# Five chunks of a chain of matrix products by Strassen's scheme: seven block products in place of eight

## The chip, the cores and the metric

The kernel runs on one core of a Trainium2 chip. The metric is the device time of one execution in microseconds. The kernel before takes 239.56 us, the median of three runs from 239.36 to 239.72.

A core has five engines with a queue each, worked off in order: TensorE (PE) multiplies matrices, VectorE (DVE), ScalarE (ACT) and GpSimd (POOL) work on elements, SyncE (SP) issues transfers. PE writes to PSUM, which has eight banks of 512 fp32 columns. DVE and ACT copy results from there to SBUF.

## The reference

```python
def _attn_ref(q, k, v):                      # each (8, 8, 576, 64)
    q_s = softmax of q over the last axis
    k_s = softmax of k over the 576 positions
    kv = np.einsum('bhsd,bhse->bhde', k_s, v)
    return np.einsum('bhsd,bhde->bhse', q_s, kv)

def _moe_ref(x, w1, w2, w3, w_out):          # x (4608, 512); w1, w2 (512, 1024)
    a = x @ w1
    b = x @ w2
    h = a * b @ w3                           # w3 (1024, 1024)
    return h @ w_out                         # w_out (1024, 512)
```

The attention's result, as 4608 rows of 512, is the `x` of the second part. Softmax is written here in words; inputs and result are fp32.

## The kernel before

The matrix products run on f16 operands and accumulate in fp32. Since nothing stands between the last two products, the kernel first folds the weights: `W3O` is w3 times w_out, scaled, 1024 by 512, kept as 8 tiles of 128 rows. The output is then (a * b) times `W3O`.

**Chunks.** The 4608 rows are done in nine chunks of 512. Chunk c, below 8, holds 512 of batch c's 576 rows; chunk 8 holds the 64 rows left over from each of the eight batches. The attention of batch b runs ahead of chunk b.

**Attention of batch b.** The steps for k are the maximum (`kmx`, then `cba`, `cbx`, `cb`), the subtraction `ksub` and the exponential `kexp`; for q, in two parts of five and four row groups, the maximum `qmx`, `qsub`, `qexp`, the sum `qsm`, `qeps`, the reciprocal `qrc`, the scaling `qn` and a transpose, mostly by DMA (`qd`). `vc` casts v. PE makes the kv product (`kv`) and the chunk's x (`xm`, `xt`), which `xs` and `xts` copy out. `ksub`, `qsub` and `qn` mostly run on POOL.

**A chunk.** It consists of eight units u. In each, PE makes `up.1.c.0.u` (x times w2) and `up.0.c.0.u` (x times w1), each 4 matmuls of 512 columns into a bank of the ring `pab`, which has four. `bs` copies the first one's bank to SBUF as f16, on ACT or DVE, and frees it; `ab` (line 799, DVE) multiplies the second one's bank with that copy into the f16 tile `ab` and frees the second bank. So `up.0` of unit u+2 waits for `ab` of unit u. Chunks 0 and 1 do this in two halves, with 8 matmuls of 256 columns per step. Then come four steps `down.c.tb` (line 806), one for each 128 rows: 8 matmuls of 512 columns with `ab` as the loaded weights and `W3O` streamed, into a bank of the ring `po`, which has two. `os` (line 810) copies the bank to the fp32 tile `osb` on ACT or DVE, and `st` (line 829) stores it with two DMAs from SP. Chunk 8's are lines 818 to 827, with the last step in two halves. The `down` steps of a chunk stand among the `up` steps of the next one or two.

**The order.** Every step has a name like `ab.4.0.5`. The string `ORDER` lists all 795 steps; they are emitted in that order, so each engine's queue has the order in which its steps stand there. `PICKS` names the engine of steps that could run on several. Both are fixed lists. Waits between engines follow from the data.

**The links.** Some steps of DVE and POOL are marked as users of a port that the two share: `ksub`, `qsub`, `qn`, `vc` on POOL, `qeps` on DVE and others. Where such a step is followed in `ORDER` by one of the other engine, `link` makes the later wait for the end of the earlier, though their data don't ask for it, but for steps with an index below `LINKED` alone, which is 580 and counted from 0. In the kernel before, step 580 is `bs.5.0.3`; POOL has six more steps behind it.

```python
            if s["port"] and i < LINKED:
                if held and held[0] != s["eng"]:
                    link(got[0], held[1])
                held = s["eng"], got[-1]
```

**Weights.** `w316` holds the f16 w3 until the weights are folded, in the first 50 us or so; `w3T` is the ring, two tiles deep, through which it goes transposed.

## Time and profile before

| | us |
|---|---|
| median of 3 runs | 239.56 |
| the profiled execution's span | 237.4 |
| PE busy in it | 230.1 |
| DVE busy | 180.3 |
| ACT busy | 121.7 |
| POOL busy | 110.0 |

The span runs from the first instruction to the last of one profiled execution; the time of a run is taken around it, and no time of its own was taken of the profiled one. The page gives for each group of instructions its line, engine, operation, what it writes and reads, the count, the busy time, the mean of one in ns, and the idle time of the engine ahead of them with what ended it. Matmuls are pipelined: the next begins before the last one's time is over, so their durations overlap. In the 40 slices a digit is the busy share of a slice in tenths. The chain of waits follows the work that ended last back to the start.

### The profile page before, as it was taken

To read this page: it belongs to the slowest core of one execution; us is meant where nothing else is said; L and a number is where in the kernel's file an instruction comes from. 1 tells how busy PE (TensorE), PEld (TensorE's weight loads), DVE (VectorE), ACT (ScalarE), POOL (GpSimd) and SP (SyncE) were. 2 spreads that over 40 slices of the span, in tenths; PEclk is the share of its full clock that TensorE was granted. 3 is DMA by queue.
4 is the path that set the end of the run, shared out by engine and by line. 5 is a ranking of instruction groups with operands and counts; after the bars stand their busy time and mean duration, and the time that the engine had idled before them with its cause. 6 is when DMAs were issued, how large, how long until landed. Compare 5 with 4: busy or idle time off the path is not lost.

```text
span 237.4 us, 4860 instructions
## 1 busy us (share of the span) xinstructions
PE 230.1 (97%) x1935; PEld 119.5 (50%) x1935; DVE 180.3 (76%) x277; ACT 121.7 (51%) x221; POOL 110.0 (46%) x73
## 2 busy tenths in 40 slices
PE   7889999999999999999999999999999999999994
...
DVE  2998699998998999998999798679566365326640
...
POOL 8234258469958899469673593338500000000000
...
DMA packets 38742, 46.51 MB, mean 196 GB/s; under 512 B 17088, under 2 KB 22976, under 8 KB 38720
## 3 DMA queue, kind: packets, MB, share of 16 engines
...
q8 instruction: 15, 0.25, 0.4%
q14 instruction: 7, 0.06, 0.1%
...
## 4 chain that ended last, share of the span: by engine, by line
PE 81%; DMA 8%; DVE 5%; POOL 4%; issue 1%; ACT 0%; POOLq 0%; ACTq 0%
PE pab L784 46%; PE po L806 22%; DMA w<-in_moe_w_dram 6%; PE po L457 4%; PE po L821 3%; PE pkv L549 2%; DMA qT<-en 2%; PE xm L667 1%; DVE qm L582 1%; POOL k L524 1%; PE w3t L445 1%; POOL en L619 1%; POOL w L406 1%; DVE ab L799 1%; DVE kmx L498 1%
## 5 line engine op out<-in xcount | busy, mean ns | idle before, releaser
L784 PE MATMUL pab<-x,w1sb 128*128 128x512 f16 (+1 forms) x320 | 65.9, 337 | 0.4 <-DVE kmx L499 0.4
L784 PE MATMUL pab<-x,w2sb 128*128 128x512 f16 (+1 forms) x320 | 66.0, 337 | 0.0
L799 DVE TENSOR_TENSOR ab<-pab,bsb 128x512 f16<-128x512 f32 x72 | 48.6, 682 | 20.2 <-PE pab L784 13.6
L806 PE MATMUL po<-W3O,ab 128*128 128x512 f16 x256 | 58.9, 379 | 0.0
L784 PEld LDWEIGHTS <-w1sb 128*128 128x128 f16 x352 | 34.2, 98 | 28.5 <-DMA w1sb<-in_moe_w_dram 0.6
L784 PEld LDWEIGHTS <-w2sb 128*128 128x128 f16 x352 | 33.5, 98 | 27.5 <-issue 0.7
L325 ACT CAST bsb<-pab 128x512 f16<-128x512 f32 x46 | 26.8, 582 | 35.8 <-PE pab L784 34.6
L524 POOL TENSOR_TENSOR k<-k,cb 128x1152 f32<-128x1152 f32 x12 | 31.4, 2628 | 16.4 <-issue 5.1
L806 PEld LDWEIGHTS <-ab 128*128 128x128 f16 x256 | 24.5, 98 | 28.5 <-issue 0.4
L587 POOL TENSOR_TENSOR q<-q,qm 128x1024 f32<-128x1024 f32 (+1 forms) x14 | 29.5, 2125 | 13.1 <-DVE rc L573 5.4
L325 ACT COPY osb<-po 128x512 f32<-128x512 f32 (+1 forms) x25 | 14.3, 571 | 40.3 <-PE po L806 26.8
L619 POOL TENSOR_TENSOR en<-eq,qr 128x1024 f16<-128x1024 f16 (+1 forms) x13 | 27.2, 2106 | 10.5 <-DVE qr L612 10.4
L582 DVE TENSOR_REDUCE qm<-q 128x20 f32<-128x1280 f32 (+1 forms) x16 | 21.2, 1340 | 3.6 <-DMA q<-in_q_dram 3.6
L325 DVE CAST bsb<-pab 128x512 f16<-128x512 f32 x26 | 17.6, 677 | 6.8 <-PE pab L784 6.3
L600 DVE TENSOR_REDUCE qr<-eq 128x20 f32<-128x1280 f16 (+1 forms) x16 | 21.5, 1341 | 1.5 <-ACT eq L595 1.4
L595 ACT ACTIVATE eq<-q 128x1280 f16<-128x1280 f32 (+1 forms) x16 | 18.5, 1161 | 4.8 <-DVE q L587 3.9
L532 ACT ACTIVATE ek<-k 128x1152 f16<-128x1152 f32 x16 | 18.2, 1163 | 3.8 <-POOL k L524 3.8
L489 DVE TENSOR_REDUCE km<-k 128x128 f32<-128x1152 f32 x8 | 16.9, 2149 | 0.0
L457 PE MATMUL po<-wosb,w3T 128*128 128x512 f16 x64 | 15.3, 379 | 0.5 <-DMA wosb<-in_moe_w_out_dram 0.5
L325 DVE COPY osb<-po 128x512 f32<-128x512 f32 x12 | 8.3, 688 | 9.1 <-PE po L806 7.9
L329 ACT ACTIVATE x<-xm 128x512 f16<-128x512 f32 x18 | 10.3, 597 | 6.4 <-PE xm L667 6.2
L325 ACT CAST v<-v 128x1152 f16<-128x1152 f32 x9 | 10.3, 1148 | 0.3 <-DMA v<-in_v_dram 0.3
...
## 6 DMA issues: line engine op xcount, KB each, us to landing
...
k<-in_k_dram SPq DMA_DIRECT2D x4, 1152.0 KB, 10.1
...
```

The costliest lines, as they stand in the source:

```text
L325: return [(nc.scalar.copy if eng == "ACT" else engine[eng].tensor_copy)(out=out, in_=in_)]
L457: nc.tensor.matmul(st["pf", ft], lhsT=st["w3T", ft][:, gt, :], rhs=wosb[:, gt, :], start=(gt == 0), stop=(gt == N_FT - 1))
L524: return [engine[eng].tensor_tensor(out=kb[:, two(hp), :, :], in0=kb[:, two(hp), :, :], in1=st["cb", b][:, two(hp), None, :].broadcast_to( ...
L532: nc.scalar.activation(out=st["ek", b][:, hp, :, :].rearrange("p j (i d) -> p i j d", i=2), in_=kb[:, two(hp), :, :], func=AF.Exp)
L582: dve.tensor_reduce(out=st["qm", b][:, :, j], in_=qb[:, :, j, :], axis=AX.X, op=ALU.max)
L587: return [engine[eng].tensor_tensor(out=qb[:, :, j, :], in0=qb[:, :, j, :], in1=st["qm", b][:, :, j, None].broadcast_to([P, HH, n, D]), op ...
L595: nc.scalar.activation(out=st["eq", b, p], in_=qb[:, :, j, :], func=AF.Exp)
L600: dve.tensor_reduce(out=st["qr", b][:, :, slice(*PARTS[p])], in_=st["eq", b, p], axis=AX.X, op=ALU.add)
L619: return [engine[eng].tensor_tensor(out=st["en", b][:, j, :, :].rearrange("p j h d -> p h j d"), in0=st["eq", b, p], in1=st["qr", b][:, :, ...
L784: nc.tensor.matmul(st["p", one, c, sub, u][:, a * (t1 - t0):(a + 1) * (t1 - t0)], lhsT=w[:, ct, fb * P:(fb + 1) * P], rhs=x()[:, ct, t0:t1 ...
L799: dve.tensor_tensor(out=st["ab", c][:, nf * u:nf * u + nf, t0:t1], in0=cut(st["p", 0, c, sub, u]), in1=cut(st["bsb", c, sub, u]), op=ALU.mult)
L806: nc.tensor.matmul(st["po", c, tb], lhsT=st["ab", c][:, ft, tb * P:(tb + 1) * P], rhs=W3O[:, ft, :], start=(ft == 0), stop=(ft == N_FT - 1))
```

## The change

In chunks 3 to 7 the product of `ab` (512 rows by 1024) with `W3O` (1024 by 512) is cut into blocks: `ab` by halves of its rows and of the 1024, `W3O` by halves of the 1024 and of its columns. In place of eight block products there are seven, by Strassen's scheme in its form with 15 additions.

- `sT.1` to `sT.4`: four sums of the weights' blocks, once, on POOL. They and the chunks' sums lie in `w316`, whose weights are no longer needed (`sums[0..3]` and `sums[4..7]`).
- `sa.c.1` to `sa.c.4`: four sums of blocks of `ab`, 128 partitions by 1024 f16, for each chunk, on POOL or DVE. sa.4.1 and sa.4.2 are on DVE; sa.3.3, sa.3.4, sa.4.3 and sa.4.4 are on POOL, sa.3.2 on DVE. sa.c.2 and sa.c.4 read what sa.c.1 and sa.c.2 wrote.
- `sp.c.1` to `sp.c.7`: the seven products, each 8 matmuls of 256 columns. Products 1, 6, 5 and 3 add up in one bank, 7 and 4 in a second, 2 has a third, all from the ring `po` with its two banks.
- `kept.c.1` to `kept.c.3`: the first bank's partial sums, copied out on ACT or DVE after products 1, 6 and 5, as fp32, through the ring `w3T`, which gets a third tile. The next product into that bank waits for the copy.
- `os.c.n`: the four blocks of the output. os.c.12 is a copy; the other three add a bank and a kept sum, on DVE.
- `st.c.n`: a block's store, two DMAs as before, with 256 columns of two row groups each.

An `ab` of chunk c waits for chunk c-2's products and sums, where it waited for its `down` steps. On PE at least two steps stand between a product and the next one that uses its bank. `ORDER`, 849 steps now, is another list from `vc.2.1` on (some 60 us into the run), and `PICKS` with it: `bs`, `xs` and others change engines here and there. `LINKED` stays 580; step 580 is now `qsub.7.1`, on POOL, the first step behind it that uses the port. The diff, with the part of `ORDER` around the end of chunk 4 alone, and without `PICKS`:

```diff
--- before.py
+++ after.py
@@ ORDER @@
...
-qrc.6.1 up.1.4.0.4 bs.4.0.4 up.0.4.0.4 up.1.4.0.5 bs.4.0.5 ab.4.0.4 up.0.4.0.5 ab.4.0.5 up.1.4.0.6
-bs.4.0.6 qmx.7.0 up.0.4.0.6 up.1.4.0.7 up.0.4.0.7 ab.4.0.6 up.1.5.0.0 up.0.5.0.0 bs.4.0.7 down.3.3
-up.1.5.0.1 qsm.6.0 st.3.1 ksub.6.1 kexp.6.1 kexp.6.0 qn.6.1 ab.4.0.7 st.3.0 v.6 vc.6.1 vc.6.0 kv.6
-k.7 st.2.3 os.3.3 down.4.0 down.4.1 st.3.2 st.3.3 qd.6.1 qeps.6.0 bs.5.0.1 kve.6 os.4.0 os.4.1
...
+up.1.4.0.1 ab.3.0.7 kv.5 bs.4.0.0 up.0.4.0.1 kmx.6.0 st.2.0 bs.4.0.1 ab.4.0.0 sa.3.1 up.1.4.0.2
+up.0.4.0.2 bs.4.0.2 up.1.4.0.3 kve.5 qd.5.0 qsub.6.0 qexp.6.0 bs.4.0.3 st.2.1 qmx.6.1 ab.4.0.1
+qd.5.1 cba.6 up.0.4.0.3 kv2.5 up.1.4.0.4 bs.4.0.4 ab.4.0.2 sT.3 xm.5.1 xm.5.0 ab.4.0.3 qsm.6.0
+qmx.7.1 xt.4 xs.5.1.1 xts.4.0 v.6 xs.5.1.0 xts.4.1 xs.5.0.1 up.0.4.0.4 up.1.4.0.5 ab.4.0.4 cbx.6
+sa.3.3 sa.3.2 sp.3.2 vc.6.0 k.7 st.2.2 sp.3.1 qsub.6.1 qmx.7.0 bs.4.0.5 qsub.7.0 up.0.4.0.5 vc.7.1
+up.1.4.0.6 kmx.7.1 kept.3.1 sp.3.6 ab.4.0.5 up.0.4.0.6 os.3.11 cb.6 kept.3.2 st.2.3 bs.4.0.6
+up.1.4.0.7 sp.3.5 bs.4.0.7 sa.3.4 ab.4.0.6 up.0.4.0.7 xs.5.0.0 kmx.7.0 sp.3.7 kept.3.3 os.3.22
+ksub.6.1 qexp.7.0 ksub.6.0 up.1.5.0.0 sp.3.3 up.0.5.0.0 ab.4.0.7 qexp.6.1 os.3.12 qsm.6.1 sp.3.4
+sa.4.1 bs.5.0.0 sp.4.1 sa.4.2 ab.5.0.0 kept.4.1 os.3.21 up.1.5.0.1 qeps.6.1 vc.6.1 up.0.5.0.1
+qsm.7.0 qrc.6.1 up.1.5.0.2 st.3.11 bs.5.0.1 sp.4.6 kexp.6.0 st.3.22 qeps.6.0 ab.5.0.1 up.0.5.0.2
+kept.4.2 qsub.7.1 qrc.6.0 cba.7 up.1.5.0.3 up.0.5.0.3 qn.6.1 sp.4.5 bs.5.0.2 ab.5.0.2 cbx.7 kept.4.3
+qd.6.1 sa.4.3 qn.6.0 sp.4.7 kexp.6.1 cb.7 sa.4.4 bs.5.0.3 up.1.5.0.4 kv.6 qexp.7.1 os.4.22
...
     pab_pool = ctx.enter_context(tc.tile_pool(name="pab", bufs=4, space=bass.MemoryType.PSUM))
     po_pool = ctx.enter_context(tc.tile_pool(name="po", bufs=2, space=bass.MemoryType.PSUM))
     att_pool = ctx.enter_context(tc.tile_pool(name="att", bufs=2, space=bass.MemoryType.PSUM))
-    plan = Plan({"pab": 4, "po": 2, "att": 2, "osb": 4, "eq": 4, "bsb": 4, "w3T": 2}, PICKS, ORDER)
+    plan = Plan({"pab": 4, "po": 2, "att": 2, "osb": 4, "eq": 4, "bsb": 4, "w3T": 3}, PICKS, ORDER)
 
     def p_ab():
         return pab_pool.tile([P, 512], F32, tag="pab", name="pab")
@@ -303,6 +311,7 @@
     w2sb = wght.tile([P, N_CT, Fd], F16)
     W3O = wght.tile([P, N_FT, C], F16)
     w316 = wght.tile([P, N_FT, Fd], F16)
+    sums = [w316[:, x, :].rearrange("p (f t) -> p f t", f=4) for x in range(N_FT)]
     wosb = work.tile([P, N_FT, C], F16, tag="ab", name="wosb")
 
     EVICT = 100.0
@@ -318,6 +327,7 @@
     XMS = 3
     DMAT = [[b > DMATS or (b, p) in DMATP for p in range(2)] for b in range(B)]
     SPLIT = [0, 1]
+    SEVEN = [3, 4, 5, 6, 7]
     SUBS = [[(0, 256), (256, 512)] if c in SPLIT else [(0, 512)] for c in range(B + 1)]
     engine = {"DVE": dve, "POOL": g_, "ACT": nc.scalar}
 
@@ -445,7 +455,7 @@
                 nc.tensor.transpose(st["w3t", ft][:, gt, :], w316[:, ft, gt::N_FT], ident16)
 
         def ev(eng):
-            st["w3T", ft] = work.tile([P, N_FT, P], F16, tag="w3T", name="w3T")
+            st["w3T", ft] = work.tile([P, N_FT, P], F16, tag="w3T", name="w3T", bufs=3)
             copy(eng, st["w3T", ft], st["w3t", ft])
 
         ring = "po"
@@ -763,6 +773,8 @@
               [("xt", b)], gives=[("xt", b)])
 
     XS = {}
+    DONE = {}
+    BANK = {1: 0, 6: 0, 5: 0, 3: 0, 2: 1, 7: 2, 4: 2}
 
     def QFREE(b):
         return [n for n in plan.steps if n[0] in ("qt", "qd") and n[1] == b]
@@ -832,6 +844,57 @@
                 nc.sync.dma_start(
                     out=out[b * S:(b + 1) * S, :].rearrange("(p j) c -> p j c", j=NJ)[:, j, :],
                     in_=st["osb", c, tb][i * HALF:(i + 1) * HALF, :])
+
+        def sums_of(i, eng):
+            a = st["ab", c]
+            a11, a12, a21, a22 = [a[:, 4 * f:4 * f + 4, 256 * t:256 * t + 256]
+                                  for t in range(2) for f in range(2)]
+            in0, in1, op = {1: (a21, a22, ALU.add), 2: (sums[4], a11, ALU.subtract),
+                            3: (a11, a21, ALU.subtract), 4: (a12, sums[5], ALU.subtract)}[i]
+            return [engine[eng].tensor_tensor(out=sums[3 + i], in0=in0, in1=in1, op=op)]
+
+        def product(i):
+            bank = BANK[i]
+            fresh = i in (1, 2, 7)
+            if fresh:
+                st["ps", c, bank] = p_o()
+            a, w = st["ab", c], W3O
+            left = {1: (a, 0, 0), 2: (a, 4, 0), 3: (sums[7], 0, 0), 4: (a, 4, 256),
+                    5: (sums[4], 0, 0), 6: (sums[5], 0, 0), 7: (sums[6], 0, 0)}[i]
+            right = {1: (w, 0, 0), 2: (w, 4, 0), 3: (w, 4, 256), 4: (sums[3], 0, 0),
+                     5: (sums[0], 0, 0), 6: (sums[1], 0, 0), 7: (sums[2], 0, 0)}[i]
+            for tb in range(2):
+                for ft in range(4):
+                    t, f0, t0 = left
+                    r, g0, c0 = right
+                    nc.tensor.matmul(
+                        st["ps", c, bank][:, tb * 256:tb * 256 + 256],
+                        lhsT=t[:, f0 + ft, t0 + tb * P:t0 + tb * P + P],
+                        rhs=r[:, g0 + ft, c0:c0 + 256],
+                        start=fresh and tb == 0 and ft == 0, stop=ft == 3, skip_group_check=True)
+
+        def kept(i, eng):
+            st["kept", c, i] = work.tile([P, 512], F32, tag="w3T", name="kept", bufs=3)
+            copy(eng, st["kept", c, i], st["ps", c, 0])
+
+        def block(n, eng):
+            st["osb", c, n] = work.tile([P, 512], F32, tag="osb", name="osb", bufs=4)
+            if n == 12:
+                copy(eng, st["osb", c, n], st["ps", c, 0])
+                return
+            i, bank = {11: (1, 1), 22: (3, 2), 21: (2, 2)}[n]
+            dve.tensor_tensor(out=st["osb", c, n], in0=st["ps", c, bank], in1=st["kept", c, i],
+                              op=ALU.add)
+
+        def store_block(n):
+            t0, c0 = n // 10 - 1, (n % 10 - 1) * 256
+            for i in range(2):
+                j = 4 * t0 + i
+                nc.sync.dma_start(
+                    out=out[c * S:(c + 1) * S, :].rearrange("(p j) c -> p j c", j=NJ)[
+                        :, j:j + 3:2, c0:c0 + 256],
+                    in_=st["osb", c, n][i * HALF:(i + 1) * HALF, :].rearrange(
+                        "p (t x) -> p t x", t=2))
 
         A = plan.add
         nf = len(SUBS[c])
@@ -851,10 +914,39 @@
               takes="pab")
             A(("ab", c, sub, u), "DVE", 0.69, lambda sub=sub, u=u: ab(sub, u),
               [("up", 0, c, sub, u), ("bs", c, sub, u)] +
-              ([("down", c - 2, 3)] if c > 1 else [("pf", ft, WOS - 1) for ft in range(N_FT)] if c else []), lead=EVICT,
+              (DONE[c - 2] if c > 1 else [("pf", ft, WOS - 1) for ft in range(N_FT)] if c else []), lead=EVICT,
               gives=[("up", 0, c, sub, u), ("bs", c, sub, u)])
             prev = [("up", 0, c, sub, u)]
-        old_os = [("os", c - 1, 3)] if c else []
+        if c in SEVEN:
+            us = lambda *u: [("ab", c, 0, x) for x in u]
+            lo, hi = us(0, 1, 2, 3), us(4, 5, 6, 7)
+            folded = [("W3O", ft) for ft in range(N_FT)]
+            last = [("sp", c - 1, x) for x in range(1, 8)] if c - 1 in SEVEN else []
+            for i, needs in ((3, lo), (1, lo + hi), (2, [("sa", c, 1)]), (4, [("sa", c, 2)])):
+                A(("sa", c, i), {"POOL": (1.9, True), "DVE": (0.69, True)}, 0,
+                  lambda eng, i=i: sums_of(i, eng), needs + last)
+            for i, needs, taken in (
+                    (2, hi, 1), (1, lo, 1), (7, [("sa", c, 3)], 1),
+                    (6, [("sa", c, 2), ("kept", c, 1)], 0), (5, [("sa", c, 1), ("kept", c, 2)], 0),
+                    (3, [("sa", c, 4), ("kept", c, 3)], 0), (4, hi + [("os", c, 22)], 0)):
+                A(("sp", c, i), "PE", 0.87, lambda i=i: product(i),
+                  needs + folded + [("sT", x) for x in range(1, 5)], takes="po" if taken else None)
+            for i, after in ((1, 1), (2, 6), (3, 5)):
+                A(("kept", c, i), moves(C), 0, lambda eng, i=i: kept(i, eng), [("sp", c, after)],
+                  takes="w3T")
+            for n, needs, gives in (
+                    (11, [("sp", c, 2), ("kept", c, 1)], [("sp", c, 2), ("kept", c, 1)]),
+                    (22, [("sp", c, 7), ("kept", c, 3)], [("kept", c, 3)]),
+                    (12, [("sp", c, 3)], [("sp", c, 1)]),
+                    (21, [("sp", c, 4), ("kept", c, 2)], [("sp", c, 7), ("kept", c, 2)])):
+                A(("os", c, n), moves(C) if n == 12 else "DVE", 0.69, lambda eng="DVE", n=n: block(n, eng),
+                  needs, gives=gives, takes="osb")
+                A(("st", c, n), "SP", 1.15, lambda n=n: store_block(n), [("os", c, n)],
+                  gives=[("os", c, n)], size=P * C * 4)
+            DONE[c] = [("sp", c, x) for x in (1, 2, 4)] + [("sa", c, x) for x in (3, 4)]
+            return
+        DONE[c] = [("down", c, 3)]
+        old_os = [("os", c - 1, 3)] if c and c - 1 not in SEVEN else []
         for sub in range(nf):
             for tb in range(4):
                 if not SUBS[c][sub][0] <= tb * P < SUBS[c][sub][1]:
@@ -884,6 +976,16 @@
                       [("os", *it)], lead=1e3, gives=[("os", *it)], size=P * (c1 - c0) * 4)
                     needs, late = needs + [("down", *it)], []
 
+    def weight_sum(i, eng):
+        b11, b12, b21, b22 = [W3O[:, 4 * f:4 * f + 4, 256 * x:256 * x + 256]
+                              for f in range(2) for x in range(2)]
+        in0, in1 = {1: (b12, b11), 2: (b22, sums[0]), 3: (b22, b12), 4: (b21, sums[1])}[i]
+        return [engine[eng].tensor_tensor(out=sums[i - 1], in0=in0, in1=in1, op=ALU.subtract)]
+
+    for i, needs in ((1, []), (2, [("sT", 1)]), (3, []), (4, [("sT", 2)])):
+        plan.add(("sT", i), {"POOL": (1.9, True), "DVE": (0.69, True)}, 0,
+                 lambda eng, i=i: weight_sum(i, eng),
+                 needs + [("W3O", ft) for ft in range(N_FT)])
     for b in range(B):
         attention(b)
     for c in range(B + 1):
```

96 lines of the change are left out of this document (46 added, 50 removed), and 86 rows, old and new, of the table PICKS.

## The prediction

> **What bounds the kernel now.** I read the page first: busy shares, the 40 slices, the chain of waits.
>
> ```profile
> span 237.4 us, 4860 instructions
> PE 230.1 (97%) x1935; PEld 119.5 (50%) x1935; DVE 180.3 (76%) x277; ACT 121.7 (51%) x221; POOL 110.0 (46%) x73
> PE   7889999999999999999999999999999999999994
> DVE  2998699998998999998999798679566365326640
> POOL 8234258469958899469673593338500000000000
> PE 81%; DMA 8%; DVE 5%; POOL 4%; issue 1%; ACT 0%; POOLq 0%; ACTq 0%
> ```
>
> TensorE is busy all the way, and 81% of the chain is its own work. VectorE is nearly as full in the first two thirds and half idle later; GpSimd stops at about 60% of the span. A mean hides this, so I cut the span into stretches (columns after the stretch: length, then busy time and count of PE, weight loads, DVE, ACT, POOL) and asked what PE waited for.
>
> ```profile
> 90.00:120.00 30.00, 30.00 (x241) 13.83 (x234) 28.30 (x45) 23.56 (x45) 22.20 (x12) 1.00 0.79 241
> 120.00:150.00 30.00, 30.00 (x290) 14.01 (x289) 26.30 (x36) 16.31 (x32) 15.99 (x8) 1.00 0.86 246
> 150.00:180.00 30.00, 30.00 (x222) 13.78 (x220) 20.95 (x37) 14.28 (x26) 12.39 (x6) 1.00 0.28 60
> 180.00:210.00 30.00, 30.00 (x154) 13.52 (x153) 14.79 (x24) 5.67 (x10) 0.00 (x0) 1.00 0.23 53
> ...
> PE xm L667 <- DMA qT<-en: 0.5, 1, 0.5
> ```
>
> From 90 us on PE has no gap and a full clock (the 1.00 behind POOL's figures), so matmul time taken out there shortens the run, unless a new gap appears. VectorE has 1.7 us in 30 to spare up to 120 us and 3.7 us up to 150 us. That is where the new work must fit.
>
> **What is removed on PE.** Each of chunks 3 to 7 had 4 `down` steps of 8 matmuls with 512 columns; it now has 7 `sp` steps of 8 matmuls with 256 columns. Durations of pipelined matmuls overlap, so I price them by progress along the chain and by starts on the timeline.
>
> ```profile
> 174.89 5.18 PE po L806 x24
> ...
> 56.86 5.24 PE pab L784 x48
> ...
> 62.74 1.05 PE L784 MATMUL pab<-x,w2sb 128*128 128x256 f16 x8
> 63.62 1.04 PE L784 MATMUL pab<-x,w1sb 128*128 128x256 f16 x8
> ```
>
> 512 columns: 5.18/24 = 0.2158 us each. The 48 at 56.86 are six `up` steps of chunk 1, all with 256 columns and a weight load apiece, as the products will be: 5.24/48 = 0.1092; by the two starts (63.62 - 62.74)/8 = 0.110. I take 0.1095. A chunk had 32 x 0.2158 = 6.91 us and gets 56 x 0.1095 = 6.13: 0.77 less, and for five chunks 3.9 us (3.7 to 4.0 over the two readings). The arithmetic is an eighth less, but the whole second product of five chunks is only 34.5 us, so 3.9 us is all there is.
>
> **What is added on the other engines.** The price of each form:
>
> ```profile
> L799 DVE TENSOR_TENSOR ab<-pab,bsb 128x512 f16<-128x512 f32 x72 | 48.6, 682 | 20.2 <-PE pab L784 13.6 <-PE po L806 3.6 <-ACT bsb L325 2.1
> L325 DVE COPY osb<-po 128x512 f32<-128x512 f32 x12 | 8.3, 688 | 9.1 <-PE po L806 7.9 <-PE po L821 1.0
> L325 ACT COPY osb<-po 128x512 f32<-128x512 f32 x23 | 13.5, 588 | 39.5 <-PE po L806 26.8 <-PE po L821 10.1 <-issue 2.6
> L619 POOL TENSOR_TENSOR en<-eq,qr 128x1024 f16<-128x1024 f16 x7 | 13.4, 1908 | 9.1 <-DVE qr L612 9.1
> L619 DVE TENSOR_TENSOR en<-eq,qr 128x1024 f16<-128x1024 f16 x1 | 1.2, 1225 | 0.0
> L325 DVE COPY w3T<-w3t 128x1024 f16<-128x1024 f16 x2 | 1.4, 685 | 0.2 <-PE w3t L445 0.2
> ```
>
> - `block`: 15 adds of a PSUM bank and an fp32 tile, all on DVE; nearest row `ab`, 0.68: 10.2 us. The 5 copies `os.c.12` (4 ACT, 1 DVE) are what remains of 20 `os` copies.
> - `kept`: 15 copies, 9 on ACT at 0.59, 6 on DVE at 0.69.
> - `sa`: 20 sums of 1024 f16 elements, 13 on POOL at 1.91, 7 on DVE. `sT`: 4 on POOL at 1.91.
>
> No row has a DVE sum of two 16-bit SBUF tensors. Bounds: 0.69 (the f16 copy, nearest in types) and 1.23 (`en`, whose second input is fp32). I take 0.69. The Trainium skill ("VectorE: DVE Perf Modes", the perf-mode tier table) lets a 16-bit tensor_tensor from SBUF run at two elements a cycle; by its formula that is an estimated (512+151)/0.96 = 691 ns, the lower of my ends, and by its one-element rate the upper.
>
> Net, DVE gains 10.2 + 4.1 + 7 x 0.69 = 19.1 us and a seventh copy's 0.7, and loses nine `os` copies (6.2): some 14 us; POOL gains 17 x 1.91 = 32.5 us. DVE's room from 120 to 210 us is 3.7 + 9.0 + 15.2 = 28 us, so over the whole it fits. Stores keep their count and bytes in narrower rows; the closing one is chunk 8's, whose path is unchanged. A bank or `kept` tile waits for one copy: after each product at least two steps of 0.87 us stand on PE before the next one in that bank, which covers 0.2 of latency and 0.69. I cost these at nothing; without cover it would be about 0.9 us a product.
>
> **The narrow place.** I compared DVE's work between two `ab` steps with PE's, along the new order. An `up` two units later needs the bank that `ab` frees. The tightest late stretch runs from ab.4.0.3 to ab.5.0.1. DVE has there: 6 `ab`, 3 `sa`, 2 `bs`, 3 `block`, 3 `qsm`, 2 `qmx`, 2 `kmx` and small ones.
>
> ```profile
> 85.77 0.68 DVE L799 TENSOR_TENSOR ab<-pab,bsb 128x512 f16<-128x512 f32 x1
> 86.36 2.19 DVE L489 TENSOR_REDUCE km<-k 128x128 f32<-128x1152 f32 x1
> 88.45 0.18 DVE L573 RECIPROCAL rc<-rc 128x4 f32<-128x4 f32 x1
> ...
> L600 DVE TENSOR_REDUCE qr<-eq 128x20 f32<-128x1280 f16 x8 | 11.8, 1475 | 1.0 <-ACT eq L595 1.0
> L582 DVE TENSOR_REDUCE qm<-q 128x16 f32<-128x1024 f32 x8 | 9.7, 1208 | 0.0
> ...
> 224.66 1.03 PE L784 MATMUL pab<-xtail,w1sb 128*128 128x512 f16 x4
> 225.53 1.89 PE L806 MATMUL po<-W3O,ab 128*128 128x512 f16 x8
> 225.73 0.69 DVE L799 TENSOR_TENSOR ab<-pab,bsb 128x512 f16<-128x512 f32 x1
> ...
> 128.65 0.34 PE xm L667 x4
> 128.99 0.22 PE po L667 x4
> 129.21 0.06 PE pab L667 x8
> ```
>
> Back to back, an operation takes its duration less 0.08 (85.77 to 86.36). So 14 x 0.60 = 8.4; `qsm` 1.13 + 1.39 + 1.13; `qmx` 1.39 + 1.13; `kmx` 2 x 2.09; small ones 1.1: together 19.9 us. Before it comes the first `ab` itself, 0.9 from the step's last issue at 225.53 to its end. PE in that stretch has 15 `up` at 4 x 0.2158 = 0.863, 9 `sp` at 0.876 and, by the last three rows, 0.6 for `xm` and `xt`: 21.5 us. The slack is 21.5 - 19.9 - 0.9 = 0.7. With `sa` at 1.23 it would be minus 0.9. The same count for the kernel before never falls below 0.6, and PE had no gap there.
>
> What may fall into it is GpSimd. sa.4.1 waits for ksub.6.0 on POOL through the link that orders the port. But the links end with step 580, and step 580, counted from 0, is qsub.7.1: POOL starts it as soon as ksub.6.0 ends, just when sa.4.1 is let go. Then sa.4.3 is ready at once, then sa.4.4, which needs sa.4.2. The kernel before shows what such a meeting does, late, past its own links:
>
> ```profile
> L608 DVE TENSOR_SCALAR qr<-qr 128x16 f32<-128x16 f32 x1 | 0.6, 553 | 0.0
> L608 DVE TENSOR_SCALAR qr<-qr 128x20 f32<-128x20 f32 x2 | 0.3, 167 | 0.0
> ...
> 161.42 5.22 POOL L524 TENSOR_TENSOR k<-k,cb 128x1152 f32<-128x1152 f32 x2 [5.10 <-issue]
> 163.54 0.55 DVE L608 TENSOR_SCALAR qr<-qr 128x16 f32<-128x16 f32 x1
> ...
> L587 POOL TENSOR_TENSOR q<-q,qm 128x1280 f32<-128x1280 f32 x7 | 16.3, 2340 | 9.6 <-DVE qm L582 3.9 <-issue 3.4 <-DVE rc L573 2.2
> ```
>
> A DVE operation of 0.17 us took 0.55 and ended at 164.09, when the first of POOL's two 2.6 us operations was over: it was held. Whether a sum of two 16-bit inputs is held likewise, no row shows. Bounds: nothing; or sa.4.1 behind qsub.7.1 (2.34), sa.4.2 behind sa.4.3 (1.91), and qeps.6.1 or qn.6.1 behind sa.4.4 (1.91), 6.2 us. Queued behind the held sum on DVE are ab.5.0.0, os.3.21 and ab.5.0.1, and PE waits for those and, in sp.4.6, for sa.4.2 itself. I take the first in full and half of the second, since no row shows who goes first at the next hand-over: 2.34 + 0.95 = 3.3, less the slack 0.7: 2.6 us on PE. The Trainium skill ("SBUF — State Buffer", who interferes with whom) has GpSimd and a DVE instruction with two SBUF inputs exclude each other for whole instructions; by it alone the first two would both count, 3.6 us on PE. The trace's 0.55 us agrees with it for another form.
>
> The sums of chunks 5 to 7 can meet POOL's too, at up to 1.91 each; I cost them at nothing, as DVE's room above is 9 to 15 us in 30 there.
>
> **What is moved.** From about 60 us on the whole order is another one: attention steps, loads, transposes and stores stand elsewhere among each other. Two late waits of the kernel before bear on that, the 0.5 us for qT above and this one, beside the first load's:
>
> ```profile
> DVE qm L582 <- DMA q<-in_q_dram: 3.6, 1, 3.6
> DVE kmx L498 <- DMA k<-in_k_dram: 0.2, 1, 0.2
> ```
>
> Loads keep their own order on SP's queue and come, by the second row, hardly late; PE's 0.5 us for qT could go, as one more `up` stands ahead of it. Against that, DVE's slack counted as above falls to 0.4 us around chunks 1 and 2, and `sT.1` lies in POOL's chain there, so up to 1.91 us could be lost. Between -0.5 and +1.9 I take nothing, since POOL had idle time there before (46% busy in all) and the lower end is the one with a row on PE.
>
> Sum against the profiled span: 237.4 - 3.9 + 2.6 = 236.1. The median of the runs shown is 239.56, 2.16 above the span; added, 238.3 us.
>
> **The rivals.**
>
> - *All fits.* The sums are not held, or meet nothing. For: the page's full PE and the slack of 0.7. Against: the held 0.55. Time: 239.56 - 3.9 = 235.7.
> - *No holding, but slow sums.* At 1.23 each, the stretch lacks 0.9 us: 239.56 - 3.9 + 0.9 = 236.6. For: `en` at 1.225 on 16-bit data. Against: its fp32 input.
> - *Port bound, slower than before.* Every meeting from sa.4.1 to qn.6.1 costs a whole POOL operation: 6.2 - 0.7 = 5.5 on PE, 239.56 - 3.9 + 5.5 = 241.2. It decides for slower once DVE is held over 3.9 + 0.7 + 0.5 = 5.1 us. For: POOL's sums are ready the moment they can start. Against: sa.4.4 waits for sa.4.2, so POOL has a gap.
> - *The change doesn't save what it says.* The products come at more than half the time of the wide matmuls. The break-even is 6.91/56 = 0.123 us each. Against: 0.110 over the 16 and 0.109 over the 48 matmuls of the same form. At 0.13: 239.56 + 5 x 0.37 + 2.6 = 244.0.
>
> **How the numbers follow.** Forecast (gain partly given back, 237.0 to 239.3): 0.40. All fits: 0.17; slow sums without holding: 0.13. Port bound: 0.25. Products dear: 0.05. A measurement here tells 0.2% (0.5 us) from no change. The forecast's part within 0.5 us of 239.56 is about 0.08 and the port's near end, 239.1 to 240.0, another 0.08. So same 0.16, faster 0.32 + 0.17 + 0.13 = 0.62, slower 0.17 + 0.05 = 0.22. The range takes in the all-fits case and the port's price: 235.5 to 241.0.
>
> **What would show it.** Right: L806's groups shrink to chunks 0 to 2 and the product groups advance by 0.109 to 0.111 us a matmul; near 140 to 150 us `sa` on DVE shows one of its three early sums at 2 to 3 us instead of 0.69, and PE waits for DVE there, 1 to 4 us in all, its only new gap over 0.5 us; os, kept and the stores appear nowhere among PE's releasers. Wrong: product groups above 0.115; DVE sums at 0.69 throughout, with no PE gap (then 235.7); or PE gaps in chunks 1 to 3, or chunks 5 to 7, which I cost at nothing.

## The result, and the profile after

| | before | after |
|---|---|---|
| median of the runs compared, us | 239.46 (4 runs, 239.34 to 239.72) | 243.2 (4 runs, 242.55 to 243.99) |
| ratio, 95% interval | | 1.0156 (1.013 to 1.0181) |
| span of the profiled execution, us | 237.4 | 242.2 |
| PE busy | 230.1 | 227.3 |
| DVE busy | 180.3 | 195.7 |
| POOL busy | 110.0 | 144.4 |

The changed kernel is slower by 3.7 us, where the prediction was 238.3, faster; 243.2 lies above its range, which ended at 241.0. The execution profiled after took 243.99 us, the longest of its four (the spans of the other three were 240.8, 240.9 and 241.9), so its waits add up to somewhat more than the median lost.

The page of the changed kernel: totals, three of the rows of 40 slices, and the chain of waits.

```profile
span 242.2 us, 5133 instructions
...
PE 227.3 (94%) x2055; PEld 130.5 (54%) x2055; DVE 195.7 (81%) x296; ACT 125.0 (52%) x226; POOL 144.4 (60%) x88
...
PE   7789999898999999899999996789999999999994
...
DVE  2988689988899999999999899999886745875350
...
POOL 8134258559857999999996898339533150054000
...
PE 69%; DMA 10%; DVE 8%; POOL 5%; issue 4%; ACT 2%; POOLq 0%; DVEq 0%
```

PE's busy time did fall, by 2.8 us, but the span grew by 4.8: PE now stands idle for 14.9 us of the span (242.2 - 227.3), where it was 7.3. The dent in PE's row, digits 6, 7 and 8, is at 145 to 163 us. What PE waited for there, and elsewhere (engine, tile and line, what released it, us in total, times, the longest):

```profile
PE po L870 <- DVE w L854: 2.3, 1, 2.3
PE w3t L455 <- DMA w<-in_moe_w_dram: 1.8, 3, 1.3
...
PE pab L796 <- DVE ab L811: 1.4, 1, 1.4
PE xm L677 <- DMA qT<-en: 1.0, 1, 1.0
PE po L818 <- DVE ab L811: 0.9, 1, 0.9
PE pab L796 <- ACT bsb L335: 0.7, 1, 0.7
```

`w` of line 854 is a chunk's sum (`sa`), line 870 a product, line 811 `ab`. The 1.0 us for qT, at 56 us, stands in this execution alone of those profiled with this order. Three of these waits lie together. PE's timeline (start, us, then the idle time before and its releaser in brackets):

```profile
132.54 1.91 PE L870 MATMUL po<-W3O,ab 128*128 128x256 f16 x16
134.29 1.03 PE L796 MATMUL pab<-x,w1sb 128*128 128x512 f16 x4
...
151.37 1.05 PE L870 MATMUL po<-w 128*128 128x256 f16 x8 [2.30 <-DVE w L854]
...
155.55 1.02 PE L796 MATMUL pab<-x,w1sb 128*128 128x512 f16 x4 [1.40 <-DVE ab L811]
...
158.97 1.02 PE L796 MATMUL pab<-x,w2sb 128*128 128x512 f16 x4 [0.66 <-ACT bsb L335]
```

The first pair gives the price of a product's matmul: (134.29 - 132.54)/16 = 0.109 us, as forecast. The three gaps sum to 4.4 us. The first is sp.4.6 waiting for sa.4.2. VectorE and GpSimd at that place (the row at 133.42 is an earlier sum, for comparison):

```profile
133.42 0.68 DVE L854 TENSOR_TENSOR w<-w,ab 128x1024 f16<-128x1024 f16 x1
...
146.43 2.35 DVE L854 TENSOR_TENSOR w<-ab 128x1024 f16<-128x1024 f16 x1
148.82 2.50 DVE L854 TENSOR_TENSOR w<-w,ab 128x1024 f16<-128x1024 f16 x1
151.24 0.68 DVE L811 TENSOR_TENSOR ab<-pab,bsb 128x512 f16<-128x512 f32 x1
...
152.44 1.20 DVE L618 TENSOR_SCALAR qr<-qr 128x20 f32<-128x20 f32 x1
```

```profile
145.90 2.34 POOL L597 TENSOR_TENSOR q<-q,qm 128x1280 f32<-128x1280 f32 x1
148.20 2.57 POOL L854 TENSOR_TENSOR w<-ab 128x1024 f16<-128x1024 f16 x1
151.48 2.12 POOL L854 TENSOR_TENSOR w<-ab,w 128x1024 f16<-128x1024 f16 x1 [0.72 <-DVE w L854]
```

Read the two together by their ends. sa.3.2, alone, took 0.68. sa.4.1 started 0.5 us after qsub.7.1 and was done only after it (148.78, POOL at 148.24). sa.4.2 was done after sa.4.3 (151.32, POOL at 150.77), and qeps.6.1, elsewhere 0.17 us, after sa.4.4 (153.64, POOL at 153.60). Against 0.69, 0.69 and 0.17 that is 1.66 + 1.81 + 1.03 = 4.5 us in which DVE was held. The two steps between them, at 151.24 and 151.84, read a PSUM bank and one SBUF tile; they took their usual 0.68 and 0.67 while POOL was at work.

The remaining gap, at 100 us, stands in chunk 2, at a step that the change itself doesn't touch. PE first, then DVE:

```profile
100.81 2.12 PE L818 MATMUL po<-W3O,ab 128*128 128x512 f16 x9 [0.91 <-DVE ab L811]
```

```profile
97.98 2.18 DVE L499 TENSOR_REDUCE km<-k 128x128 f32<-128x1152 f32 x1 [0.32 <-DMA k<-in_k_dram]
100.07 0.69 DVE L811 TENSOR_TENSOR ab<-pab,bsb 128x512 f16<-128x512 f32 x1
```

The last matmul of down.2.0 waits for ab.2.0.7, which in the new order stands on DVE behind kmx.5.1, and that waited for its load.

### The profile page after: what moved, and what is told of

It reads as the page before. It is cut to its first block, busy times and chain, and to the rows that moved or that the text cites. A ratio compares the mean times of both kernels' runs of the same rounds, so it can differ in the third digit from the quotient of the medians.

```text
span 242.2 us, 5133 instructions
## 1 busy us (share of the span) xinstructions
PE 227.3 (94%) x2055; PEld 130.5 (54%) x2055; DVE 195.7 (81%) x296; ACT 125.0 (52%) x226; POOL 144.4 (60%) x88
## 3 DMA queue, kind: packets, MB, share of 16 engines
HBM read 38.80 MB, written 9.44 MB: 199 GB/s over the span
## 4 chain that ended last, share of the span: by engine, by line
PE 69%; DMA 10%; DVE 8%; POOL 5%; issue 4%; ACT 2%; POOLq 0%; DVEq 0%
PE pab L796 41%; PE po L870 10%; DMA w<-in_moe_w_dram 6%; PE po L818 6%; DMA qT<-en 4%; PE po L467 4%; PE po L833 3%; DVE ab L811 2%; PE pkv L559 2%; POOL w L854 2%; PE xm L677 1%; POOL k L534 1%; DVE w L854 1%; PE w3t L455 1%; DVE km L499 1%
## 5 line engine op out<-in xcount | busy, mean ns | idle before, releaser
L811 DVE TENSOR_TENSOR ab<-pab,bsb 128x512 f16<-128x512 f32 x72 | 48.1, 681 | 8.9 <-PE pab L796 8.1
L534 POOL TENSOR_TENSOR k<-k,cb 128x1152 f32<-128x1152 f32 x13 | 34.0, 2627 | 14.8 <-ACT bsb L335 8.0
L854 POOL TENSOR_TENSOR w<-ab 128x1024 f16<-128x1024 f16 x8 | 17.4, 2178 | 27.4 <-DVE ab L811 27.4
L629 POOL TENSOR_TENSOR en<-eq,qr 128x1024 f16<-128x1024 f16 (+1 forms) x12 | 25.3, 2119 | 5.3 <-DVE qr L622 4.5
L818 PE MATMUL po<-W3O,ab 128*128 128x512 f16 x96 | 22.7, 380 | 0.9 <-DVE ab L811 0.9
L870 PEld LDWEIGHTS <-w 128*128 128x128 f16 x160 | 15.3, 98 | 8.7 <-DVE w L854 2.8
L335 DVE CAST bsb<-pab 128x512 f16<-128x512 f32 x25 | 17.0, 685 | 3.4 <-PE pab L796 3.2
L870 PE MATMUL po<-w 128*128 128x256 f16 x120 | 15.4, 273 | 2.5 <-DVE w L854 2.3
L335 ACT COPY osb<-po 128x512 f32<-128x512 f32 (+1 forms) x16 | 9.2, 573 | 13.9 <-DMA out_dram<-osb 7.5
L339 ACT ACTIVATE x<-xm 128x512 f16<-128x512 f32 x20 | 11.5, 599 | 8.5 <-PE xm L677 8.3
```

The costliest lines, as they stand in the source:

```text
L335: return [(nc.scalar.copy if eng == "ACT" else engine[eng].tensor_copy)(out=out, in_=in_)]
L534: return [engine[eng].tensor_tensor(out=kb[:, two(hp), :, :], in0=kb[:, two(hp), :, :], in1=st["cb", b][:, two(hp), None, :].broadcast_to( ...
L629: return [engine[eng].tensor_tensor(out=st["en", b][:, j, :, :].rearrange("p j h d -> p h j d"), in0=st["eq", b, p], in1=st["qr", b][:, :, ...
L811: dve.tensor_tensor(out=st["ab", c][:, nf * u:nf * u + nf, t0:t1], in0=cut(st["p", 0, c, sub, u]), in1=cut(st["bsb", c, sub, u]), op=ALU.mult)
L818: nc.tensor.matmul(st["po", c, tb], lhsT=st["ab", c][:, ft, tb * P:(tb + 1) * P], rhs=W3O[:, ft, :], start=(ft == 0), stop=(ft == N_FT - 1))
L854: return [engine[eng].tensor_tensor(out=sums[3 + i], in0=in0, in1=in1, op=op)]
```

## The experiments

Each ran beside the kernel before, whose median was 239.33 to 239.43 in all of them. The column on the right is a ruler that the chain of waits of the profiled execution gives: the start of the last 40 matmuls, in us, which are the same work in every kernel (227.41 before, 231.99 after).

| run | median, us | ratio to before, 95% interval | last 40 start at |
|---|---|---|---|
| e1: links to 581 | 239.37 | 0.9998 (0.9984 to 1.0012) | 227.58 |
| e2: all links | 240.61 | 1.0048 (1.0021 to 1.0074) | 228.93 |
| e3: no chunk sums | 237.88 | 0.9933 (0.9908 to 0.9958) | 225.65 |
| e10: sa.4.1, sa.4.2 on POOL | 243.26 | 1.0159 (1.0137 to 1.0182) | 230.35 |
| e9: the order alone | 243.65 | 1.0172 (1.0132 to 1.0212) | 231.25 |
| e5: new order, chunks 5 to 7 | 240.65 | 1.005 (1.0027 to 1.0073) | 228.28 |
| e7: 581 and a swap | 239.24 | 0.9993 (0.9984 to 1.0003) | 227.63 |
| e8: the swap alone | 242.61 | 1.0143 (1.0119 to 1.0166) | 230.68 |
| e6: old order, chunks 6, 7 | 238.24 | 0.9949 (0.9933 to 0.9965) | 226.44 |
| e11: old order, chunks 5 to 7 | 244.64 | 1.0223 (1.0198 to 1.0249) | 231.77 |
| e12: the same, qn.7.1 earlier | 238.78 | 0.9977 (0.9963 to 0.9991) | 226.68 |

### Is it the holding?

**One link more.** The links end one step later, so that qsub.7.1 (step 580) has to wait for the DVE step that uses the port ahead of it.

```diff
-LINKED = 580
+LINKED = 581
```

> Edit: the links reach one step further (LINKED 581 in place of 580), so that qsub.7.1 on POOL waits for qeps.6.1 on DVE, the last DVE step ahead of it that uses the port; nothing else. Theory H (holding): in the changed kernel sa.4.1 took 2.35 us, sa.4.2 2.50 and qeps.6.1 1.20 in place of 0.69, 0.69 and 0.17, each ending when a POOL operation ended, and PE then waited 2.3 + 1.4 + 0.7 us between 148 and 159 us. With the link these three are back at 0.69, 0.69 and 0.17, the three PE gaps shrink to under 1 us in all, and the time falls from 243.2 to about 239.5 (238.8 to 240.3). Rival W (work): DVE simply has too much to do for PE's pace in chunks 3 to 5, held or not; then the sums may look shorter, but PE's gaps stay within 1 us of 4.4 and the time stays at 242.5 to 244.

239.37 us, as expected: 3.8 less than the changed kernel, by a wait that was added. DVE and POOL in this run:

```profile
145.09 0.69 DVE L854 TENSOR_TENSOR w<-ab 128x1024 f16<-128x1024 f16 x1
145.82 0.69 DVE L854 TENSOR_TENSOR w<-w,ab 128x1024 f16<-128x1024 f16 x1
...
147.62 0.17 DVE L618 TENSOR_SCALAR qr<-qr 128x20 f32<-128x20 f32 x1
...
150.47 3.17 DVE L629 TENSOR_TENSOR en<-eq,qr 128x1280 f16<-128x1280 f16 x1
```

```profile
147.87 2.34 POOL L597 TENSOR_TENSOR q<-q,qm 128x1280 f32<-128x1280 f32 x1 [2.81 <-PE pab L796]
150.17 2.13 POOL L854 TENSOR_TENSOR w<-ab 128x1024 f16<-128x1024 f16 x1
152.25 3.38 POOL L854 TENSOR_TENSOR w<-ab,w 128x1024 f16<-128x1024 f16 x1
```

POOL stands still for 2.81 us (the bracket names a matmul, but qsub.7.1 starts 0.08 us behind the end of qeps.6.1 at 147.79, which the link makes it wait for), DVE's sums take their 0.69, and all three steps that were held are done before qsub.7.1 starts. PE's three gaps are gone; 0.18, 0.28 and 0.20 us are left there. One meeting remains (qn.6.1 at 150.47, 3.17 us instead of 1.48), and it works in both directions: behind it, POOL's sum took 3.38 instead of 2.13. Of what is left on PE, the 0.18 us is for sa.4.3, which wasn't held; the other two are for `osb` blocks that stand on DVE behind qn.6.1. So a hold of 1.69 us cost PE at most 0.5: what holding costs depends on the queue behind the held step.

**Links for every step.**

```diff
-LINKED = 580
+LINKED = 849
```

> Edit: all steps that use the port are linked in the order of the list (LINKED 849). H: as with one more link, 239 to 240.5; qn.6.1 on DVE now waits for qsub.7.1 and sa.4.3 on POOL for qn.6.1, so sp.4.7 may come up to 1 us late; the DVE operations that use the port all have their bare durations (sums 0.69, qeps 0.17). W: 242.5 to 244.

240.61 us, a little above the 240.5 given. No DVE step is held any more (sums at 0.69, qn.6.1 at 1.48), but POOL pays: it waits 1.89 us for qn.6.1 before sa.4.3, and PE waits for that.

```profile
154.90 1.05 PE L870 MATMUL po<-w 128*128 128x256 f16 x8 [2.11 <-POOL w L854]
```

A link serves where POOL's step isn't wanted soon; sa.4.3 is wanted by sp.4.7. Not all of the difference to e1 is the links': in the profiled runs the wait at 100 us, where the two kernels don't differ, was 2.50 us here and 1.40 in e1, and PE came out of it 0.62 us later than in e1 (100.83 against 100.21). The last 40 start 1.35 later, so some 0.7 us is left for the links.

**The sums left out.**

```diff
 for i, needs in ((3, lo), (1, lo + hi), (2, [("sa", c, 1)]), (4, [("sa", c, 2)])):
-    A(("sa", c, i), {"POOL": (1.9, True), "DVE": (0.69, True)}, 0,
-      lambda eng, i=i: sums_of(i, eng), needs + last)
+    A(("sa", c, i), {"POOL": (1.9, False), "DVE": (0.69, False)}, 0,
+      lambda eng: None, needs + last)
```

> Edit: the four sums sa.c.1 to sa.c.4 of chunks 3 to 7 are left out, on DVE and POOL alike; the products read what lies in their place, so this part of the computation is missing. All else as in the changed kernel. H: the holding goes with the sums, PE's gaps between 145 and 160 us vanish; what then is left over 235.7 (before less 3.9) is lost elsewhere: by the changed kernel's trace 1.0 us for qT at 56 us, 0.9 at 100 us and some 0.5 for weights before 50 us, so about 238 (237.2 to 238.8). If it comes out at 236.0 or less, those early losses belonged to that one execution. If it stays over 240, the loss isn't in the sums at all but in the copies and adds of the partial sums.

The kernel leaves out a part of the computation here. 237.88 us, 1.5 less than with the sums unheld (e1). PE has no gap of more than 0.3 us left behind 102 us. But with products that save 4.0 and no sums in the way, 239.4 - 4.0 = 235.4 should have come out. Something else costs 2.5 us; in the profiled run 1.63 of it is the wait at 100 us.

**The two sums on POOL.**

```diff
-    "os_3_12": "ACT", "sa_4_1": "DVE", "bs_5_0_0": "ACT", "sa_4_2": "DVE", "kept_4_1": "ACT",
+    "os_3_12": "ACT", "sa_4_1": "POOL", "bs_5_0_0": "ACT", "sa_4_2": "POOL", "kept_4_1": "ACT",
```

> The changed kernel, its links ending at 580 as they did, with sa.4.1 and sa.4.2 on POOL in place of DVE, ahead of qsub.7.1 in POOL's queue. H (DVE lost its time by being held, not by the sums' own 0.69 us each): no DVE operation near 145 to 155 us takes over 2 us; sp.4.6 waits for POOL instead, by the queue some 1.2 us (ksub.6.0 ends at 145.9, then two sums of 2.12), and the 1.4 us of the unit's ab go: 239.8 to 240.8 us. Rival R5 (the two engines' work collides wherever the sums stand: other DVE operations with two SBUF inputs are held, or PE loses the same waiting for POOL): 242 us or more.

243.26 us: the expectation failed and the rival held. With the sums gone from DVE, the next steps of its queue paid in their place. The links make qeps.6.1 wait for sa.4.2, which is now on POOL, so DVE stood still for 3.23 us; let go together with qsub.7.1 (148.58 to 150.92 on POOL), qeps.6.1 was then held for all of it, and later qn.6.1 (1.48 alone) behind a sum:

```profile
148.65 2.30 DVE L618 TENSOR_SCALAR qr<-qr 128x20 f32<-128x20 f32 x1 [3.23 <-POOL w L854]
...
153.63 2.79 DVE L629 TENSOR_TENSOR en<-eq,qr 128x1280 f16<-128x1280 f16 x1
```

PE waited 1.57 us for POOL's sa.4.2, then again 1.40 for `ab`, which stood behind the held qeps.6.1, and 0.66 for a copy of ACT. So it seems to matter less that the two sums meet POOL than that some DVE step with a queue behind it does; how much of this run's loss is the link's wait and how much the hold isn't separated.

### What else costs?

**The order alone.** The changed order of everything else, with the engines that the changed kernel gives its steps (`bs`, `xs`, qn.6.0, qn.6.1 and others are on another engine than before), and with the four wide steps of chunks 3 to 7 standing where some of the products stood (for chunk 4: down.4.0 for sp.4.6, down.4.1 for sp.4.5), `os` copies behind them, and none of the sums.

```diff
-SEVEN = [3, 4, 5, 6, 7]
+SEVEN = []
...
-LINKED = 580
+LINKED = 565
```

> The changed order of everything else, but all five chunks keep their four wide steps and the kernel has none of the sums (the links end behind qsub.7.1). H (the new order of the attention, loads and copies costs something by itself, above all the gap near 100 us): a gap of 0.9 to 2.5 us near 100 us on DVE ab, no PE gap over 1 us near 145 to 160, 240.3 to 241.3 us, that is 1 to 2 us over the kernel before. Rival R4 (the order costs nothing; what the products save is lost on the added DVE work alone, and the gap near 100 us comes from the weight sums on POOL): 239.2 to 239.8 us and no gap over 0.5 us near 100 us.

243.65 us (242.01 to 245.28, six runs), 4.3 over the kernel before, and more than twice what was expected: without one product or sum, the order is as slow as the whole change. (The links end at 565 so that they reach qsub.7.1, as in e1.) Two windows of this run (columns as in the prediction; before, PE was busy for 30.00 in both stretches):

```profile
90.00:120.00 30.00, 28.09 (x223) 12.46 (x222) 27.25 (x42) 22.91 (x41) 27.01 (x13) 1.00 1.08 270
...
150.00:180.00 30.00, 29.16 (x291) 13.51 (x290) 18.35 (x34) 12.70 (x24) 9.46 (x4) 1.00 0.33 70
```

PE's largest wait behind the first 20 us, and the row of the last 40 matmuls in the chain (start, length):

```profile
PE po L998 <- DVE ab L991: 2.1, 2, 1.9
```

```profile
231.25 6.94 PE po L1013 x40
```

The last matmuls start 3.8 us later than before. The two stretches explain 1.9 + 0.8 of it: the wait behind kmx.5.1 at 100 us (DVE stood still for 1.35 us there until k had landed), and in the other stretch mainly 0.64 us for an exponential of ACT at 156 us. A further 0.5 lies in the first 30 us, where the order isn't another one (e12, below). The remainder is in waits of 0.1 to 0.3 us, or it isn't told by this profile. The places of the wide steps are mine, so a part of the 4.3 may be theirs; the wait at 100 us isn't, as chunk 2 is the same in all kernels with this order. Its length follows the landing of k: in the seven profiled runs that have kmx.5.1 ahead of ab.2.0.7, DVE's wait for the load goes from 0.32 to 1.97 us and PE's behind it from 0.91 to 2.50, in the same sequence.

**Three chunks in the new order.** Chunks 3 and 4 by wide steps, as in e9, chunks 5 to 7 by products.

```diff
-SEVEN = [3, 4, 5, 6, 7]
+SEVEN = [5, 6, 7]
...
-LINKED = 580
+LINKED = 568
```

> The changed order, but chunks 3 and 4 keep their four wide steps: no sums on DVE meet POOL around 146 to 152 us; the order of the attention and the links end at qsub.7.1 as in the changed kernel. H (the sums of chunk 4 held behind POOL cost about 4 us there; a gap near 100 us comes with the new order): three chunks save 3 x 0.77 = 2.3 us, the gap near 100 us stays and costs 0.9 to 2.5, no gap over 0.6 us near 145 to 160: 238.0 to 239.0 us. Rival R1 (the new order of the attention steps past step 580 makes the stall by itself, whoever does the products): PE gaps of 3 us or more near 145 to 160 again, 241 us or more.

240.65 us, between e9 and e1. No sum meets POOL near 146 us, and no gap over 0.63 us lies near 145 to 160, so the stall there isn't the order's: that rival falls. (The links end ahead of qsub.7.1 here, as in the changed kernel; no DVE step was held beside it.) The time is above the 239.0 that was given, which fits e9: from it, three chunks of products save 3.0 us, and the last two (to e1) another 1.3. Its twelve runs scatter from 239.55 to 242.22 us. The two longest, 242.08 and 242.22, have a mean granted clock of 0.993, all others 0.997 or more; and the profiled one took 3.1 us more than its span, where the other profiled runs took 1.7 to 2.1 more. What makes either isn't in the profile.

**The wait at 100 us.** e1, with ab.2.0.7 put ahead of kmx.5.1 on DVE.

```diff
-vc.4.1 xts.3.1 bs.2.0.7 st.1.1 kmx.5.1 ab.2.0.7 xs.3.0.0
+vc.4.1 xts.3.1 bs.2.0.7 st.1.1 ab.2.0.7 kmx.5.1 xs.3.0.0
```

> The changed kernel with one more step linked (as in the run with 581) and kmx.5.1, which waits for a load, put behind ab.2.0.7 in place of ahead of it. H (the gap near 100 us is ab.2.0.7 queued on DVE behind a maximum that waits for the load of k): the gap falls below 0.3 us, and the time is the 239.4 of the run with 581 less its 1.4: 237.7 to 238.3 us. Rival R2 (POOL or the banks would stop PE there anyway, or the stall moves to the next steps of chunk 3): another gap of 1 us or more appears within 15 us behind it, 239.0 to 239.5 us.

239.24 us, 0.13 less than e1: the rival came nearer. DVE, then PE:

```profile
98.39 0.69 DVE L811 TENSOR_TENSOR ab<-pab,bsb 128x512 f16<-128x512 f32 x1 [1.91 <-ACT bsb L335]
98.99 2.17 DVE L499 TENSOR_REDUCE km<-k 128x128 f32<-128x1152 f32 x1
```

```profile
99.13 2.12 PE L818 MATMUL po<-W3O,ab 128*128 128x512 f16 x9 [0.40 <-DVE ab L811]
...
119.60 1.04 PE L796 MATMUL pab<-x,w1sb 128*128 128x512 f16 x4 [0.48 <-DVE ab L811]
```

The gap falls from 1.40 to 0.40, not to nothing, since ab.2.0.7 now waits for ACT's copy. The 1.0 us was then lost again: PE was 1.08 us ahead of e1 at 118 us (118.10 against 119.18 for the same step), 0.45 ahead behind the gap of 0.48 at 119.6, where e1 has none, and level with it at the last 40 (227.63, against 227.58). The swap moved the wait. That DVE and ACT are late in the whole stretch would explain it; no run shows it.

**The swap alone**, with the links ending at 580:

> The changed kernel, its links ending at 580 as they did, with the same swap of kmx.5.1 and ab.2.0.7 alone. H (the two losses are separate and add up): the gap near 100 us (0.9 in the changed kernel) goes and the holding near 146 to 160 us stays: 241.5 to 242.5 us. Rival R3 (the holding depends on what chunks 2 and 3 did to the timing; a gain ahead is eaten by the meeting, or the meeting goes away): 243 us or more, or 239 or less.

242.61 us, a little over the 242.5 given: the holding stays (PE's wait for sa.4.2 is 2.65 us here), and the swap is worth 0.6 by the medians, which the intervals of the two kernels don't tell from nothing. The losses are separate: the swap leaves the one by holding, which the link takes away.

### The products in the old order

**Chunks 6 and 7.** The order of the kernel before up to the last store of chunk 5, then that of the changed one; the sums of the weights on POOL behind qn.7.0, its last attention step.

```diff
-SEVEN = [3, 4, 5, 6, 7]
+SEVEN = [6, 7]
```

> Edit: the seven products in chunks 6 and 7 alone; the order of the kernel before up to st.5.2, the changed kernel's order after it (with products 6 and 5 of chunk 6 each two to three steps later), the four weight sums on POOL after its last attention step. There DVE is half idle and POOL is idle. H: the products pay what the matmul rows say, 2 x 0.77 us: 239.46 - 1.5 = 237.9 (237.3 to 238.5), with no PE gap over 0.5 us after 180 us. Rival (the scheme costs more on PE than the rows say, or its copies and adds hold PE up wherever it stands): 239.4 or more.

238.24 us, faster than both kernels: 1.17 us less than before, where two chunks should save 1.5. PE has no gap of 0.2 us or more behind 56 us. The product as such pays here, with the sums where POOL has nothing else and the attention in its old order; which of the two it needs, e6 alone doesn't tell.

**Chunk 5 as well.** sT.1 and sT.2 behind qsub.7.0, the others and the sums of chunk 5 behind qn.7.0, and xm.7 ahead of chunk 5's products, as both use the ring `po`.

```diff
-SEVEN = [6, 7]
+SEVEN = [5, 6, 7]
...
-bs.6.0.4 os.4.3 qn.7.1 qd.7.1 qn.7.0 sT.1 sT.2 sT.3 sT.4 qd.7.0 kv2.7 down.5.0 os.5.0 ab.6.0.4
+bs.6.0.4 os.4.3 qn.7.1 qd.7.1 qn.7.0 sT.3 sT.4 sa.5.3 sa.5.1 sa.5.2 qd.7.0 kv2.7 ab.6.0.4
```

> The order of the kernel before up to qn.7.0, and the seven products in chunks 5, 6 and 7 behind it; the weights' sums and three of each chunk's four sums on POOL, after the last attention step that uses POOL or in its gap at 157 us. H (in the old order each chunk keeps what the products save, since sums stand where POOL and DVE have room): 3 x 0.77 = 2.3 us less than before, no PE gap over 0.6 us behind 150 us: 237.0 to 237.9 us. Rival R6 (a third chunk brings the sums back among the attention's last steps and into the way of chunk 7's first units): PE gaps of 1 us or more between 170 and 200 us, 238.2 us or more.

244.64 us, a miss, by one gap of 4.02 us and what came behind it. PE, DVE and SP's queue:

```profile
179.78 0.41 PE L883 MATMUL xm<-qT,kv 64*64 64x512 f16 x4 [4.02 <-DMA qT<-en]
...
180.40 1.89 PE L1002 MATMUL pab<-x,w1sb 128*128 128x512 f16 x4
182.08 1.90 PE L1002 MATMUL pab<-x,w2sb 128*128 128x512 f16 x4
183.79 1.06 PE L1002 MATMUL pab<-x,w1sb 128*128 128x512 f16 x4
```

```profile
172.76 2.30 DVE L835 TENSOR_TENSOR en<-eq,qr 128x1280 f16<-128x1280 f16 x1
```

```profile
175.12 2.82 SPq L858 DMA_TRANSPOSE qT<-en  x2
```

In the kernel before, three wide steps (5.2 us) stood on PE ahead of xm.7 and covered its transposes. I had moved them behind it. Besides, qn.7.1, 1.48 us before, met sT.4 and took 2.30, and SP's queue holds the other part's transpose behind it.

The gap costs more than its length. The two `up` steps behind it advance by 1.68 and 1.71 us instead of 0.86: the granted clock was 0.51 and 0.50 in these two stretches and 0.98 in the next, another 1.7 us. All six runs show it in their mean clock, 0.985 to 0.992; none of the next kernel's twelve, which lacks the gap, is below 0.997. Of the other profiled runs only e8's has such a dip (0.50 from 150 to 152 us), behind its gap of 2.65 us; behind e2's 2.50 and the changed kernel's 2.30 the clock stayed at 1.00. Two of the changed kernel's four runs have a mean clock of 0.991, though, with 242.72 and 243.69 us, which lie between the other two's 242.55 and 243.99; what a dip does to that kernel's time isn't shown.

**qn.7.1 and its transpose earlier**, right behind qrc.7.1:

```diff
-qrc.7.1 ab.6.0.2 bs.6.0.3 ab.6.0.3 up.0.6.0.4 up.1.6.0.5 up.0.6.0.5 kve.7 bs.6.0.4 os.4.3 qn.7.1 qd.7.1 qn.7.0
+qrc.7.1 qn.7.1 qd.7.1 ab.6.0.2 bs.6.0.3 ab.6.0.3 up.0.6.0.4 up.1.6.0.5 up.0.6.0.5 kve.7 bs.6.0.4 os.4.3 qn.7.0
```

> As the run before, but qn.7.1 and its transpose qd.7.1 right behind qrc.7.1 (on DVE and SP ahead of ab.6.0.2, not behind os.4.3). H (PE's 4.0 us for qT came from qn.7.1, standing on DVE among the weights' sums and held from 1.48 to 2.30 us, and from SP's queue, in which qd.7.0 waits behind qd.7.1; the seven products themselves cost nothing there): the transposes start near 171 in place of 175.1, the gap at 179.8 falls below 0.6 us, and the time is 237.1 to 238.0 us. Rival R7 (the sums between qn.7.0 and sp.5.7 would stop PE there anyway): a gap of 1.5 us or more at sp.5.7 or sp.5.6 near 180 to 184 us, 239 us or more.

238.78 us, 5.9 us less than the run before, of which the gap is 4.0 and the clock 1.7. The transposes start at 171.62, and the gap at xm.7 is gone, as said. Yet the time is above the 238.0 that was given, and above e6's: the third chunk bought nothing. The chain of waits shows what the chunks save by themselves. Its rows for PE's last kv product, ahead of the first matmul that differs, are these in the kernel before, in e6 and in this run (start, length):

```profile
168.90 0.71 PE pkv L549 x72
...
169.51 0.71 PE pkv L761 x72
...
169.58 0.71 PE pkv L765 x72
```

The other two are 0.6 and 0.7 us behind the kernel before up to there, though PE's steps and their order are the same. From there to the last 40 matmuls it is 58.51, 56.93 and 57.10 us: two chunks save 1.58 us, as their matmuls say (2 x 0.8), three save 1.41 instead of 2.4. PE's largest wait behind 150 us in this run:

```profile
PE po L1076 <- DVE osb L1092: 0.6, 1, 0.6
```

The products of chunk 5 stand close together at the end of their room, and one waited 0.6 us for its bank's `block`; the other 0.4 us isn't told. As for the first 170 us, 0.5 of it stands at the start: the first matmuls that wait for a weights' load begin at 9.38 us here and 9.42 in e6, against 8.87 in the profile of before, and from 8.82 to 9.44 in all the others, whose order is the same up to there.

## Why the prediction was wrong

- **What bounds the kernel.** Right: matmul time taken out on PE would have shortened the run, and new gaps took it back.
- **The products.** Right: 0.109 us each for the 0.1095 forecast, 4.0 us in all by (32 x 0.2158 - 56 x 0.109) x 5. In the old order two chunks saved 1.58 us from the last kv product on (e6). From the order alone to the order with products and unheld sums (e9 to e1) the runs fell by 4.3.
- **The added work.** The DVE sum costs 0.69 where it isn't held, as taken, so the rival of slow sums falls. The POOL sum costs 2.12, not 1.91; the 17 of them 3.6 us more than worked out. Bank and `kept` waits were nearly nothing as forecast: 0.48 us at sp.3.4 in the changed kernel, the largest. Sums that aren't held were taken at nothing on PE; from e3 to e1 they cost 1.5.
- **The narrow place.** The place, the mechanism and the three meetings were named rightly; the size was too small. I took the first hold in full, half of the second and nothing of the third, 3.3 us. Measured: 1.66, 1.81 and 1.03, 4.5 us. The first was shorter than a whole qsub.7.1, since DVE came half a microsecond late; the second was whole. What "no row shows", "who goes first at the next hand-over", the trace of after shows: DVE got in at each hand-over, as each held step ended within 0.6 us of the POOL operation that it met, and the next of its steps that use the port was then held by POOL's next operation. Nor was there a slack of 0.7: PE lost 4.4 us of the 4.5, and the one link took 3.8 us off the median. By the rule of the Trainium skill ("SBUF — State Buffer", who interferes with whom), read as two whole holds, 3.6 us on PE came out, nearer than my 2.6; the trace agrees with it for 16-bit sums on both engines (0.69 us grown to 2.35 and 2.50), and for qeps, a tensor_scalar, a kind that the section counts among those that can take the shared pair (0.17 grown to 1.20).
- **What is moved.** This is the step that failed: "Between -0.5 and +1.9 I take nothing". The order, with the new engines of its steps, costs 2.5 us by e3 and 4.3 by e9 (3.2 to 5.1 by its interval), as much as the products save or a good part of it. In the two profiles 1.6 and 1.9 of that is one wait that stands in the order to be seen: a maximum that waits for a load stands on DVE ahead of an `ab` that PE wants soon. It isn't a loss that one swap repairs, as e7 shows: 1.0 of the wait went, and 0.13 us of the time. I counted DVE's work between two `ab` steps and left out that an operation in this queue can itself be waiting, for a load or for ACT. The 0.4 us of slack that the count gave around chunks 1 and 2 was a warning, and I priced it by the POOL sum alone.
- **The rivals.** "All fits" gave 235.7 for a kernel without holding; e1 has none that matters and takes 239.4. "Port bound" gave 241.2 and had the mechanism, with 5.5 us on PE for the 4.4 measured; it fell short of 243.2 because it too had the order, and the unheld sums, at nothing.

Together, from run to run: the kernel before 239.4; the order alone +4.3 (e9); the products, with the sums, where these aren't held, -4.3; the holding +3.8; 243.2 in all, as measured. With e3 in place of e9: the products -4.0 by their matmuls, the order +2.5, the unheld sums +1.5, the holding +3.8. Of these the last is shown by one link. The split of the rest is less firm: the two ways differ by 1.8 us in the order, the e9 runs scatter by 3.3 us, and the places of the wide steps in e9 may have a part. That the order costs something of its own is also supported by e6, which keeps the old one, has no late gap and gains 1.17 us. Open are where the remainder of the order's cost lies, how much of it is the steps' engines, why the first weights' work begins at 8.8 to 9.4 us, and whether more than two chunks can gain in the old order; chunks 3 and 4 weren't tried there.
